# Moving a gate recurrence, weight conversions and one group's key and query transposes in an mLSTM and SwiGLU kernel

## The chip, the cores and the metric

One core of one Trainium2 chip runs the whole program. The metric is device microseconds of one execution; lower is better. TensorE (PE) multiplies, VectorE (DVE), ScalarE (ACT) and GpSimd (POOL) do the rest, and two engines issue transfers here: SyncE (SP) nearly all, ACT a few. "PEld" is the loading of stationary operands into PE, which overlaps PE's own work.

## The reference, cut to what matters

```python
# q, k, v, o_gate: (4, 8, 768, 40); i_gate, f_gate: (4, 8, 768)
for t in range(S):                                   # S = 768
    m_new  = np.maximum(f_gate[:, :, t] + m, i_gate[:, :, t])
    f_stab = np.exp(f_gate[:, :, t] + m - m_new)
    i_stab = np.exp(i_gate[:, :, t] - m_new)
    C = f_stab * C + i_stab * outer(v_t, k_t)        # 40 x 40 per head
    n = f_stab * n + i_stab * k_t
    y[:, :, t] = sigmoid(o_gate_t) * (C @ q_t) / max(|n . q_t|, 1)
x = y laid out as (3072 tokens, 320)
out = (silu(x @ w_gate) * (x @ w_val)) @ w_out       # d_ff = 1536
```

The weights arrive as 64-bit floats and are brought to 32 bits inside the kernel.

## The kernel before

The sequence of 768 steps is cut into six groups of 128 steps (`NG`, `g` or `n` counts them). For each group the recurrent cell is computed in parallel form, which gives 512 token rows (4 batches of 128), and these go through the SwiGLU block: `hidden(g, m)` makes chunk m of 12 of the hidden layer (20 recorded matrix products into two PSUM banks, a Silu on ACT, a product on DVE, line L640), and `project` or `project_all` multiplies by `w_out`. The cell of group n+1 is computed between the chunks of group n: a table `slots` says what is emitted after which chunk. The schedule is manual: each engine runs its instructions in the order in which the Python code emits them. An engine that waits holds back all that was emitted later for it.

The names that the change and the prediction touch:

- **Gates of the later groups.** `late_sums` (L269) makes running sums of the forget gate and the differences to the input gate; `late_maxima` (L276) makes the running maxima `M_sb` by a scan, then the decays `step1` (an Exp on ACT, L281), and stores `M_sb` to HBM as `M_dram`. From there `weights_load` spreads it into `w_sb`. `late_turns` (L604) transposes the results into `g_T`, `e_T`; `decay_rows`, `decay` make the table `dec`.
- **Weights.** `piece_load(p)` (L136) loads piece p of `PIECES`: pieces 0 and 1 hold chunk 0 and chunk 1, pieces 2 to 6 hold chunks 2-3, 4-5, 6-7, 8-9, 10-11, pieces 7 to 9 hold `w_out`. A gate half goes by SP, a value half by ACT (L142). Landing places are two `raw` buffers, or for some pieces `h_sb` and `wo_sb`, not yet used. `convert(j)` is `scale` (two ACT instructions, L186 and L188), `join` (two DVE instructions, L195, L196) and `rounded` (L203, on POOL or DVE). `ahead[m]` lists the chunks converted while chunk m is made; j = 12 to 17 are pieces of `w_out`.
- **Scores and states.** `turn` (L297) transposes keys and queries of a group on PE, with copies out of PSUM by ACT and DVE. `turn_squares` (L314) does the same for groups 3 to 5 by DVE, from tiles of 32x32 that `load_squares` (L305) fetches in 16 small transfers. `weights_sub`, `weights_mask`, `weights_exp` prepare the decay weights, `weigh_values` the weighted values, `sig` the output gate. `add` (L343) makes the sums of keys and values of a 64-step half, `next_state` (L355) decays the state on POOL and adds the sum on DVE. `attend` (L362) and `gather` use it.
- **PSUM.** Two sets of four banks: "cell" for all cell work, "gen" for `hidden` and the projection. `hidden` of chunk m+2 can start only when Silu and product of chunk m have emptied their banks.
- **Transfer counters.** Transfers issued by SP and ACT take turns on eight completion counters. An issue first waits for the landing of the transfer that last used its counter, if its engine has not yet seen that landing.

The end of the first group's work is emitted so (L736 to L742): `project_all(0, after)`, in which the table `after` says what follows which m, and then

```python
    weights_exp(0)
    weights_exp(1)
    sig(0)
    sig(1)
    weigh_values(G, 0)
    weigh_values(G, 1)
```

`result` copies each projection from PSUM by ACT to one of two `z_sb` buffers (L644), and SP stores it.

Of the kernel before, what the change touches and what calls it, by code (L numbers as in the profile page):

```python
# [18 lines left out]
L = 128  # L19
# [5 lines left out]
def kernel(  # L25
# [47 lines left out]
    def flat(t):  # L73
        return t.rearrange("p c t -> p (c t)")
# [61 lines left out]
    def piece_load(p, home=None):  # L136
        kind, m, n = PIECES[p]
        if kind == "gv":
            a, d = NKC, n * 128
            src = [(slice(i * HP, (i + 1) * HP), w[:, m * 128:(m + n) * 128].rearrange("(c p) f -> p c f", p=HP))  # L140
                   for i, w in enumerate((moe_w_gate, moe_w_val))]
            queues = (nc.sync, nc.scalar)  # L142
        else:
            a, d = n, DM
            src = [(slice(0, 128), moe_w_out[m * 128:(m + n) * 128].rearrange("(a p) d -> p a d", p=128))]
            queues = (nc.sync,)
        if src[0][1].dtype == F32:
# [12 lines left out]
        for (r, w), queue in zip(src, queues):  # L160
            queue.dma_start(out=raw[r].rearrange("p (a d) -> p a d", a=a), in_=w.bitcast(U32))  # L161
# [107 lines left out]
    def late_sums():  # L269
        nc.vector.tensor_tensor_scan(flat(f_sb), flat(keep1), flat(f_sb), 0.0, op0=ALU.mult, op1=ALU.add)  # L270
        nc.gpsimd.memset(step1, 0.0)
        nc.vector.tensor_sub(i_sb, i_sb, f_sb)
        nc.vector.tensor_copy(step1[:, 0:1, 0:1], f0[0:BH, end].unsqueeze(1))
        nc.vector.tensor_copy(step1[:, 1:, 0:1], f_sb[:, 0:NL - 1, last])

    def late_maxima():  # L276
        nc.vector.tensor_tensor_scan(flat(M_sb), flat(step1), flat(i_sb), M0[0:BH, end], op0=ALU.add, op1=ALU.max)
        nc.vector.tensor_add(m_in[:, 0:1], M0[0:BH, end].unsqueeze(1), f0[0:BH, end].unsqueeze(1))
        nc.vector.tensor_add(m_in[:, 1:], M_sb[:, 0:NL - 1, last], f_sb[:, 0:NL - 1, last])
        nc.vector.tensor_sub(step1, m_in.to_broadcast([BH, NL, SUB]), M_sb)  # L280
        nc.scalar.activation(step1, step1, AF.Exp)  # L281
        nc.sync.dma_start(out=M_dram, in_=flat(M_sb))

    M_dram = tc.dram_tile([BH, S - L], F32, name="M_dram")

# [54 lines left out]
    def small(name, n=UA):  # L340
        return bank(name)[:, 0:n * D1].rearrange("p (a d) -> p a d", d=D1)

    def add(P):  # L343
        ps = [small("add") for _ in range(2)]
        for a in range(UA):
            for i, two in QUAD:
                h = P * UH + 2 * a + two
                nc.tensor.matmul(ps[i][half(two), a, :], lhsT=k_sb[half(i), h, :], rhs=vw_sb[half(i), h, :],  # L348
                                 start=True, stop=True)
        return ps  # L350

    def state(s):
        return C_ring[s % 3]

    def next_state(s, P, ps):  # L355
        a = slice(P * UA, (P + 1) * UA)
        nc.gpsimd.tensor_tensor(state(s + 1)[:, a], state(s)[:, a],  # L357
                                dec[:, s - 2, a].unsqueeze(2).to_broadcast([128, UA, D1]), op=ALU.mult)
        nc.vector.tensor_tensor(state(s + 1)[:, a], state(s + 1)[:, a], ps, op=ALU.add)  # L359
# [215 lines left out]
    first_scores(1)
    sig(0)
    sig(1)
    piece_load(2, h_sb[:, NH - NKC:])
    piece_load(3, wo_sb)
    burn(3)  # L580
    first_own(2)
    first_own(3)
# [87 lines left out]
    def do_weigh(P):  # L670
        weigh(P, live.pop(("sp", P)))

    def do_add():
        for P in range(2):
            live["add", P] = add(P)

    def do_state(s, P):
        for i, ps in enumerate(live.pop(("add", P))):
            next_state(s + i, P, ps)
# [15 lines left out]
    def load_all(dst, a, n):  # L695
        for P in range(2):
# [3 lines left out]


    on_vector = (9, 10, 11)
    ahead = {m: [m + 2] for m in range(NFC)}
    ahead[8] = [10, 11]
    ahead[9] = []
    slots = {
        0: [run(first_state, 1, A), run(load_all, k_sb, k, 1), run(load_all, q_sb, q, 1)],
        1: [run(late_maxima), run(piece_load, 6, h_sb[:, NH - NKC:])],
        2: [run(weights_load, 1), run(load_all, v_sb, v, 1), run(decay_rows)],
        3: [run(late_turns)],  # L710
        4: [run(decay)],
        5: [run(turn, 0, (A, A), (A, V))],
        6: [run(turn, 1, (A, A), (A, V)), run(piece_load, 7)],
        7: [run(weights_sub, 1, 0), run(weights_sub, 1, 1), run(weights_mask, 0), run(weights_mask, 1)],
        8: [run(weights_exp, 0), run(weights_exp, 1), run(weigh_values, G, 0), run(weigh_values, G, 1),
            run(piece_load, 8)],
        9: [run(do_scores), run(do_weigh, 0), run(do_weigh, 1), run(load_all, o_sb, o_gate, 1)],
        10: [run(do_add), run(do_state, 2, 0), run(do_state, 2, 1)],
        11: [run(do_attend, 1, 0), run(do_gather, 1, 0, False), run(piece_load, 9)],
    }  # L720
    for m in range(NFC):
        hidden(0, m, [run(convert, j, V if j in on_vector else None) for j in ahead[m]])
        for f in slots.get(m, ()):
            f()
    after = {
        0: [run(do_attend, 1, 1), run(convert, 14), run(sig, 0), run(sig, 1), run(do_gate, 0)],
        1: [run(do_gather, 1, 1), run(weights_load, 2), run(load_all, v_sb, v, 2)],
        2: [run(do_divide, 1, 0), run(convert, 15)],
        3: [run(do_divide, 1, 1), run(load_all, k_sb, k, 2), run(load_all, q_sb, q, 2), run(load_all, o_sb, o_gate, 2)],
        4: [run(convert, 16), run(seam, 1, 0, (A, V, A, V))],  # L730
        5: [run(seam, 1, 1, (A, V, A, V))],
        6: [run(convert, 17)],
        8: [run(weights_sub, 2, 0), run(weights_mask, 0)],
        9: [run(weights_sub, 2, 1), run(weights_mask, 1)],
    }
    project_all(0, after)  # L736
    weights_exp(0)
    weights_exp(1)
    sig(0)
    sig(1)  # L740
    weigh_values(G, 0)
    weigh_values(G, 1)  # L742
    early_scope.close()
    late = ctx.enter_context(tc.tile_pool(name="late", bufs=1))
    xTs.append(late.tile([128, NKC, TW], F32, name="xT1"))
# [6 lines left out]
    for g in range(1, NG):  # L752
        n, f = g + 1, g + 2
        slots = {m: [] for m in range(NFC)}
        if n < NG:
            slots[0] = [run(turn, 0, (A, V), (A, V))] if n == 2 else [run(turn_squares, q_sq, qT)]
            slots[1] = [run(turn, 1, (A, V), (A, V))] if n == 2 else [run(turn_squares, k_sq, kT)]
            if n == 2:
                slots[1].append(run(nc.gpsimd.memset, q_sb, 0.0))
            slots[3] = [run(do_scores), run(do_weigh, 0)]  # L760
            slots[4] = [run(do_weigh, 1)]
            slots[5] = [run(do_add), run(do_state, 2 * n, 0)]
            slots[6] = [run(do_state, 2 * n, 1)]
# [58 lines left out]
```

## Time and profile before

| | us |
|---|---|
| median of 3 runs | 568.58 |
| lowest, highest | 565.74, 569.22 |
| the profiled execution | 567.32 |
| its span in the profile | 565.2 |
| DVE busy | 225.4 |
| ACT busy | 139.3 |
| POOL busy | 103.8 |

The profile is one execution; the 2.1 us between its time and its span lie outside the recorded instructions. A group of instructions is given as line, engine, operation, output<-inputs and count. "Idle before" is the time an engine stood still just before an instruction, with what released it. PE is busy nearly everywhere in this kernel, so the short stretches in which it isn't, and those in which it is busy longer than the same work takes elsewhere, are what to look for.

### The profile page before, as it was taken

To read this page: it belongs to the slowest core of one execution; us is meant where nothing else is said; L and a number is where in the kernel's file an instruction comes from. 1 tells how busy PE (TensorE), PEld (TensorE's weight loads), DVE (VectorE), ACT (ScalarE), POOL (GpSimd) and SP (SyncE) were. 2 spreads that over 40 slices of the span, in tenths; PEclk is the share of its full clock that TensorE was granted. 3 is DMA by queue.
4 is the path that set the end of the run, shared out by engine and by line. 5 is a ranking of instruction groups with operands and counts; after the bars stand their busy time and mean duration, and the time that the engine had idled before them with its cause. 6 is when DMAs were issued, how large, how long until landed. Compare 5 with 4: busy or idle time off the path is not lost.

```text
span 565.2 us, 11653 instructions
## 1 busy us (share of the span) xinstructions
PE 554.4 (98%) x5055; PEld 322.7 (57%) x5056; DVE 225.4 (40%) x379; ACT 139.3 (25%) x208; POOL 103.8 (18%) x95
## 2 busy tenths in 40 slices
PE   8997999999999999999999999999999999999997
PEld 4855545665555476455566455567455557544475
DVE  5775576880334531434612424613432631011100
ACT  4365446435401015110104201104211010111100
POOL 2132344555211123002105001206001100000000
PEclk9999999999999999999999999999999999999999
DMA  9999991594362395353295253196000131000000
GB/s 124 182 271 187 179 264 22 151 152 95 41 79 26 50 148 110 44 53 49 38 149 111 41 66 49 31 145 110 24 2 2 26 59 46 12 1 1 1 23 24
DMA packets 211227, 45.05 MB, mean 80 GB/s; under 512 B 201736, under 2 KB 206344, under 8 KB 211176
## 3 DMA queue, kind: packets, MB, share of 16 engines
q1 hardware_dynamic: 208596, 40.14, 44.5%
q10 hardware_dynamic: 2580, 4.16, 3.3%
q8 instruction: 40, 0.66, 0.5%
q14 instruction: 11, 0.09, 0.1%
HBM read 35.03 MB, written 4.01 MB: 69 GB/s over the span
## 4 chain that ended last, share of the span: by engine, by line
PE 84%; DMA 5%; SPq 4%; DVE 3%; ACT 2%; POOL 1%; issue 1%; ACTq 0%; DVEq 0%; POOLq 0%
PE gv_ps L634 49%; PE o_ps L650 23%; PE o_ps L657 5%; SPq L113 3%; DMA raw<-in_moe_w_val_dram 3%; DMA h_sb<-in_moe_w_gate_dram 2%; PE intra L372 2%; PE inter L367 2%; PE sp L327 1%; PE add L348 1%; DVE wgv_sb L196 1%; DVE wgv_sb L195 1%; POOL C L357 1%; PE tp_kq L292 0%; SPq L161 0%
## 5 line engine op out<-in xcount | busy, mean ns | idle before, releaser
L634 PE MATMUL gv_ps<-xT,wgv_sb 64*128 64x512 f32 x1440 | 320.7, 596 | 4.5 <-POOL wgv_sb L203 3.6
L634 PEld LDWEIGHTS gv_ps<-xT,wgv_sb 64*128 64x128 f32 x1440 | 144.5, 188 | 158.9 <-issue 149.4
L640 DVE TENSOR_TENSOR h_sb<-sg,gv_ps 128x512 f32<-128x512 f32 x72 | 49.4, 687 | 227.7 <-ACT sg L639 227.7
L650 PE MATMUL o_ps<-wo_sb,h_sb 128*128 128x320 f32 x480 | 130.5, 433 | 0.0
L650 PEld LDWEIGHTS o_ps<-wo_sb,h_sb 128*128 128x128 f32 x480 | 90.8, 190 | 41.0 <-issue 3.8
L639 ACT ACTIVATE sg<-gv_ps 128x512 f32<-128x512 f32 x72 | 43.0, 597 | 261.3 <-PE gv_ps L634 261.3
L357 POOL TENSOR_TENSOR C<-C,dec 128x328 f32<-128x328 f32 x20 | 14.5, 737 | 146.6 <-DVE C L359 146.6
L446 POOL TENSOR_SCALAR_AFFINE_SELECT w_sb<-w_sb 64x1024 f32<-64x1024 f32 x20 | 28.2, 1409 | 58.9 <-DVE w_sb L441 58.0
L644 ACT COPY z_sb<-o_ps 128x320 f32<-128x320 f32 x24 | 10.2, 424 | 101.8 <-PE o_ps L650 90.7
L657 PE MATMUL o_ps<-wo_sb,h_sb 128*128 128x320 f32 x96 | 26.9, 437 | 0.0
L393 POOL TENSOR_TENSOR o_sb<-o_sb,y_sb 128x640 f32<-128x640 f32 x10 | 14.2, 1425 | 61.7 <-DVE y_sb L384 61.7
L441 DVE TENSOR_TENSOR w_sb<-g_T,w_sb 128x1024 f32<-128x1024 f32 x10 | 13.1, 1354 | 26.8 <-DMA w_sb<-M_dram 26.8
L657 PEld LDWEIGHTS o_ps<-wo_sb,h_sb 128*128 128x128 f32 x96 | 17.9, 190 | 7.2
L416 DVE STREAM_TRANSPOSE xT<-x_sq 128x640 f32<-128x640 f32 x16 | 12.5, 821 | 23.5 <-DMA x_sq<-x_sb 23.5
L384 DVE TENSOR_TENSOR y_sb<-y_sb,intra 64x328 f32<-64x328 f32 x40 | 19.7, 493 | 0.7
L203 POOL TENSOR_TENSOR wgv_sb<-wgv_sb,low 128x640 int32<-128x640 int32 x8 | 13.3, 1667 | 29.2 <-DVE wgv_sb L196 29.2
L337 POOL TENSOR_TENSOR vw_sb<-v_sb,w_sb 128x656 f32<-128x656 f32 x10 | 13.0, 1318 | 8.6 <-issue 6.4
L367 PEld LDWEIGHTS inter<-C,qT 64*64 64x64 f32 x640 | 10.2, 134 | 7.3 <-issue 6.1
L359 DVE TENSOR_TENSOR C<-C,add 128x328 f32<-128x328 f32 x20 | 9.9, 493 | 10.5 <-POOL C L357 10.5
L203 POOL TENSOR_TENSOR wo_sb<-wo_sb,low 128x640 int32<-128x640 int32 x6 | 10.2, 1706 | 15.0 <-DVE wo_sb L196 10.5
L334 DVE TENSOR_TENSOR w_sb<-sp,w_sb 128x512 f32<-128x512 f32 x20 | 12.7, 682 | 0.2 <-issue 0.2
L372 PE MATMUL intra<-v_sb,w_sb 64*64 64x41 f32 x640 | 12.3, 228 | 0.4 <-DVE C L359 0.3
(127 smaller groups left out, 353.1 us busy)
## 6 DMA issues: line engine op xcount, KB each, us to landing
w_sb<-M_dram SPq DMA_DIRECT2D x10, 512.0 KB, 6.8
x_sq<-x_sb SPq DMA_DIRECT2D x128, 40.0 KB, 2.0
k_sb<-in_k_dram SPq DMA_DIRECT2D x12, 320.0 KB, 5.9
v_sb<-in_v_dram SPq DMA_DIRECT2D x12, 320.0 KB, 7.0
o_sb<-in_o_gate_dram SPq DMA_DIRECT2D x12, 320.0 KB, 5.6
raw<-in_moe_w_out_dram SPq DMA_DIRECT2D x3, 1280.0 KB, 7.8
out_dram<-z_sb SPq DMA_DIRECT2D x24, 160.0 KB, 1.8
q_sb<-in_q_dram SPq DMA_DIRECT2D x6, 320.0 KB, 8.7
```

Source lines behind the costliest of these rows:

```text
L113: nc.sync.dma_start(out=dst[:, heads(P), 0:D], in_=tokens(a, c, P))
L203: (eng or nc.gpsimd).tensor_tensor(dst, dst, lo, op=ALU.add)
L357: nc.gpsimd.tensor_tensor(state(s + 1)[:, a], state(s)[:, a], dec[:, s - 2, a].unsqueeze(2).to_broadcast([128, UA, D1]), op=ALU.mult)
L367: nc.tensor.matmul(inter[two][half(i), a, :], lhsT=qT[half(two), P * UA + a, half(i)], rhs=state(2 * n + i)[half(two), P * UA + a, :], sta ...
L372: nc.tensor.matmul(intra[i][half(c), a, :], lhsT=w_sb[half(i), h, :], rhs=v_sb[half(i), h, :], start=True, stop=True)
L384: nc.vector.tensor_tensor(t, t, intra[i][half(c)], op=ALU.add)
L446: nc.gpsimd.affine_select(w, w, compare_op=ALU.is_ge, fill=NEG, base=0, pattern=[[0, UH], [1, SUB]], channel_multiplier=-1)
L634: nc.tensor.matmul(ps[i], lhsT=wgv_sb[half(i), m, PAIRS[kc][i] if g < 2 else kc, :], rhs=x[half(i), kc, :], start=(kc == 0), stop=(kc == N ...
L639: nc.scalar.activation(sg, ps[0], AF.Silu)
L640: nc.vector.tensor_tensor(hid(g, m), sg, ps[1], op=ALU.mult)
L650: nc.tensor.matmul(p, lhsT=hid(g, m)[:, ts(u, L)], rhs=wo_sb[:, m, :], start=(m == 0), stop=(m == NFC - 1))
L657: nc.tensor.matmul(ps[u], lhsT=hid(g, m)[:, ts(u, L)], rhs=wo_sb[:, m, :], start=(m == 0), stop=(m == NFC - 1))
```

## The change

It moves work between slots and queues and changes how one group's keys and queries are transposed:

1. `late_sums` and a cut `late_maxima` (up to the scan) move ahead, among the first group's cell steps; a new `late_decay` with the Exp stands where `late_sums` stood; the difference `i_sb` moves from DVE to POOL; the store to `M_dram` is issued after piece 3.
2. Piece 6's value half is issued by SP. `ahead` converts chunks 7 to 10 one step earlier and takes the pair 10, 11 apart; `late_turns`, `decay`, `weights_sub`, `weights_mask` move up by a slot.
3. Group 2 ("third group") no longer uses `turn`: `q` and `k` come by `load_squares` (16 transfers each) and `turn_squares`; `k_sb` is still loaded, for `add`.
4. `add` for groups 2 to 5 uses 40 stationary columns in place of 64, and `next_state` then adds two ranges of 40 partitions. The decay of the first half is made ahead of the sums.
5. `weights_exp`, `sig` and `weigh_values` of group 2 move from behind `project_all(0)` into it (`after[9]`, `after[10]`).

```diff
-            queues = (nc.sync, nc.scalar)
+            queues = (nc.sync, nc.scalar if p < 6 else nc.sync)
...
-        nc.vector.tensor_sub(i_sb, i_sb, f_sb)
+        nc.gpsimd.tensor_sub(i_sb, i_sb, f_sb)
+
+    def late_maxima():
         nc.vector.tensor_copy(step1[:, 0:1, 0:1], f0[0:BH, end].unsqueeze(1))
         nc.vector.tensor_copy(step1[:, 1:, 0:1], f_sb[:, 0:NL - 1, last])
-
-    def late_maxima():
         nc.vector.tensor_tensor_scan(flat(M_sb), flat(step1), flat(i_sb), M0[0:BH, end], op0=ALU.add, op1=ALU.max)
+
+    def late_decay():
...
         nc.scalar.activation(step1, step1, AF.Exp)
-        nc.sync.dma_start(out=M_dram, in_=flat(M_sb))
...
+    def feats(i):
+        return slice(i * SUB, i * SUB + D)
...
-    def add(P):
+    def add(n, P):
         ps = [small("add") for _ in range(2)]
+        rows, w = (half, DP) if n == 1 else (feats, D)
...
-                nc.tensor.matmul(ps[i][half(two), a, :], lhsT=k_sb[half(i), h, :], rhs=vw_sb[half(i), h, :],
+                nc.tensor.matmul(ps[i][rows(two), a, :], lhsT=k_sb[half(i), h, 0:w], rhs=vw_sb[half(i), h, :],
...
-    def next_state(s, P, ps):
+    def decayed(s, P):
         a = slice(P * UA, (P + 1) * UA)
         nc.gpsimd.tensor_tensor(state(s + 1)[:, a], state(s)[:, a],
...
-        nc.vector.tensor_tensor(state(s + 1)[:, a], state(s + 1)[:, a], ps, op=ALU.add)
+
+    def next_state(s, P, ps):
+        a = slice(P * UA, (P + 1) * UA)
+        for r in (slice(0, 128),) if s < 4 else (feats(0), feats(1)):
+            c = state(s + 1)[r, a]
+            nc.vector.tensor_tensor(c, c, ps[r], op=ALU.add)
...
     first_own(0)
+    late_sums()
...
     piece_load(1)
+    late_maxima()
     first_own(1)
     first_values(1)
+    first_scores(1)
     first_x(1)
-    first_scores(1)
...
     piece_load(3, wo_sb)
+    nc.sync.dma_start(out=M_dram, in_=flat(M_sb))
...
-    late_sums()
+    late_decay()
...
-    ahead = {m: [m + 2] for m in range(NFC)}
-    ahead[8] = [10, 11]
-    ahead[9] = []
+    ahead = {m: [m + 2] for m in range(4)}
+    ahead.update({4: [6], 5: [7, 8], 6: [9], 7: [10], 8: [11], 9: [], 10: [], 11: []})
...
-        1: [run(late_maxima), run(piece_load, 6, h_sb[:, NH - NKC:])],
-        2: [run(weights_load, 1), run(load_all, v_sb, v, 1), run(decay_rows)],
-        3: [run(late_turns)],
-        4: [run(decay)],
+        1: [run(piece_load, 6, h_sb[:, NH - NKC:]), run(decay_rows)],
+        2: [run(late_turns), run(weights_load, 1), run(load_all, v_sb, v, 1)],
+        3: [run(decay)],
...
-        7: [run(weights_sub, 1, 0), run(weights_sub, 1, 1), run(weights_mask, 0), run(weights_mask, 1)],
+        6: [run(turn, 1, (A, A), (A, V)), run(weights_sub, 1, 0), run(weights_mask, 0), run(piece_load, 7)],
+        7: [run(weights_sub, 1, 1), run(weights_mask, 1), run(nc.gpsimd.memset, q_sb, 0.0)],
...
+        9: [run(do_scores), run(do_weigh, 0), run(do_weigh, 1), run(do_decayed, 2), run(load_all, o_sb, o_gate, 1)],
+        10: [run(do_add, 1), run(do_state, 2), run(rounded, 12), run(load_squares, q_sq, q, 2)],
...
+    def early_squares(part):
+        if part == 0:
+            live["k_sq"] = conv.tile([128, 4 * NKC * 128], F32, name="raw")[:, 0:PP * L].rearrange("p (a t d) -> p a t d", a=PP, d=SQ)
+            nc.gpsimd.memset(live["k_sq"], 0.0)
+            load_squares(live["k_sq"], k, 2)
+        else:
+            turn_squares(live.pop("k_sq"), kT)
...
-        3: [run(do_divide, 1, 1), run(load_all, k_sb, k, 2), run(load_all, q_sb, q, 2), run(load_all, o_sb, o_gate, 2)],
+        3: [run(do_divide, 1, 1), run(load_all, o_sb, o_gate, 2), run(early_squares, 0)],
...
+        5: [run(seam, 1, 1, (A, V, A, V)), run(convert, 17), run(weights_sub, 2, 0), run(weights_mask, 0)],
+        7: [run(weights_sub, 2, 1), run(weights_mask, 1), run(load_all, k_sb, k, 2)],
+        8: [run(turn_squares, q_sq, qT)],
+        9: [run(weights_exp, 0), run(weights_exp, 1), run(weigh_values, G, 0), run(weigh_values, G, 1)],
+        10: [run(sig, 0), run(sig, 1)],
+        11: [run(early_squares, 1)],
     }
     project_all(0, after)
-    weights_exp(0)
-    weights_exp(1)
-    sig(0)
-    sig(1)
-    weigh_values(G, 0)
-    weigh_values(G, 1)
...
-            slots[0] = [run(turn, 0, (A, V), (A, V))] if n == 2 else [run(turn_squares, q_sq, qT)]
-            slots[1] = [run(turn, 1, (A, V), (A, V))] if n == 2 else [run(turn_squares, k_sq, kT)]
-            if n == 2:
-                slots[1].append(run(nc.gpsimd.memset, q_sb, 0.0))
+            if n > 2:
+                slots[0] = [run(turn_squares, q_sq, qT)]
+                slots[1] = [run(turn_squares, k_sq, kT)]
...
-            slots[5] = [run(do_add), run(do_state, 2 * n, 0)]
-            slots[6] = [run(do_state, 2 * n, 1)]
+            slots[4].append(run(do_decayed, 2 * n))
+            slots[5] = [run(do_add, n), run(do_state, 2 * n)]
```

More of the change, by code (lines that the diff above doesn't have):

```diff
@@ L671, in do_weigh, with do_add, do_state, do_decayed @@
         weigh(P, live.pop(("sp", P)))
-    def do_add():
+    def do_add(n):
         for P in range(2):
[L675 to L679, printed above, removed]
+            live["add", P] = add(n, P)
+    def do_state(s):
+        ps = [live.pop(("add", P)) for P in range(2)]
+        for i in range(2):
+            for P in range(2):
+                next_state(s + i, P, ps[P][i])
+                if i == 0:
+                    decayed(s + 1, P)
+    def do_decayed(s):
+        for P in range(2):
+            decayed(s, P)
     def do_attend(n, P):
@@ L702 @@
     on_vector = (9, 10, 11)
-    ahead = {m: [m + 2] for m in range(NFC)}
-    ahead[8] = [10, 11]
-    ahead[9] = []
+    ahead = {m: [m + 2] for m in range(4)}
+    ahead.update({4: [6], 5: [7, 8], 6: [9], 7: [10], 8: [11], 9: [], 10: [], 11: []})
     slots = {
         0: [run(first_state, 1, A), run(load_all, k_sb, k, 1), run(load_all, q_sb, q, 1)],
-        1: [run(late_maxima), run(piece_load, 6, h_sb[:, NH - NKC:])],
-        2: [run(weights_load, 1), run(load_all, v_sb, v, 1), run(decay_rows)],
-        3: [run(late_turns)],
-        4: [run(decay)],
+        1: [run(piece_load, 6, h_sb[:, NH - NKC:]), run(decay_rows)],
+        2: [run(late_turns), run(weights_load, 1), run(load_all, v_sb, v, 1)],
+        3: [run(decay)],
         5: [run(turn, 0, (A, A), (A, V))],
-        6: [run(turn, 1, (A, A), (A, V)), run(piece_load, 7)],
-        7: [run(weights_sub, 1, 0), run(weights_sub, 1, 1), run(weights_mask, 0), run(weights_mask, 1)],
+        6: [run(turn, 1, (A, A), (A, V)), run(weights_sub, 1, 0), run(weights_mask, 0), run(piece_load, 7)],
+        7: [run(weights_sub, 1, 1), run(weights_mask, 1), run(nc.gpsimd.memset, q_sb, 0.0)],
         8: [run(weights_exp, 0), run(weights_exp, 1), run(weigh_values, G, 0), run(weigh_values, G, 1),
             run(piece_load, 8)],
-        9: [run(do_scores), run(do_weigh, 0), run(do_weigh, 1), run(load_all, o_sb, o_gate, 1)],
-        10: [run(do_add), run(do_state, 2, 0), run(do_state, 2, 1)],
+        9: [run(do_scores), run(do_weigh, 0), run(do_weigh, 1), run(do_decayed, 2), run(load_all, o_sb, o_gate, 1)],
+        10: [run(do_add, 1), run(do_state, 2), run(rounded, 12), run(load_squares, q_sq, q, 2)],
         11: [run(do_attend, 1, 0), run(do_gather, 1, 0, False), run(piece_load, 9)],
@@ L721 @@
     for m in range(NFC):
-        hidden(0, m, [run(convert, j, V if j in on_vector else None) for j in ahead[m]])
+        first = [run(convert, j, V if j in on_vector else None) for j in ahead[m]]
+        first += {10: [run(scale, 12), run(join, 12)], 11: [run(convert, 13)]}.get(m, [])
+        hidden(0, m, first)
         for f in slots.get(m, ()):
             f()
+    def early_squares(part):
[5 more added lines that the diff above has]
+            turn_squares(live.pop("k_sq"), kT)
     after = {
@@ L728 @@
         2: [run(do_divide, 1, 0), run(convert, 15)],
-        3: [run(do_divide, 1, 1), run(load_all, k_sb, k, 2), run(load_all, q_sb, q, 2), run(load_all, o_sb, o_gate, 2)],
+        3: [run(do_divide, 1, 1), run(load_all, o_sb, o_gate, 2), run(early_squares, 0)],
         4: [run(convert, 16), run(seam, 1, 0, (A, V, A, V))],
[L731 to L734, printed above, removed]
+        5: [run(seam, 1, 1, (A, V, A, V)), run(convert, 17), run(weights_sub, 2, 0), run(weights_mask, 0)],
[4 more added lines that the diff above has]
+        11: [run(early_squares, 1)],
     }
     project_all(0, after)
-    weights_exp(0)
-    weights_exp(1)
-    sig(0)
-    sig(1)
-    weigh_values(G, 0)
-    weigh_values(G, 1)
     early_scope.close()
```

## The prediction

> **What bounds the kernel now.** I read the page's chain of waits first, then the waits of PE alone, then PE's timeline around each wait, then stages with their clock. The chain by engine:
>
> ```profile
> PE 84%; DMA 5%; SPq 4%; DVE 3%; ACT 2%; POOL 1%; issue 1%; ACTq 0%; DVEq 0%; POOLq 0%
> ```
>
> In order of time its last 420 us (from 146.05) are PE alone, in rounds of 86.7 us; the rest of the 16% lies before 146. So only that first part, and PE's own work, can give time. PE's waits in 0 to 200 us (waiter, releaser: total, times, longest; after 200 there is none):
>
> ```profile
> PE gv_ps L634 <- POOL wgv_sb L203: 3.6, 1, 3.6
> PE burn L459 <- DVE warm L220: 1.2, 1, 1.2
> PE gv_ps L634 <- DVE h_sb L640: 0.5, 1, 0.5
> ...
> PE tp_kq L292 <- ACT kT L117: 0.4, 1, 0.4
> PE intra L372 <- DVE C L359: 0.3, 1, 0.3
> PE tp_kq L292 <- DVE qT L119: 0.2, 1, 0.2
> ```
>
> The largest is chunk 4's wait for its weights. ACT's timeline (start, length) shows why they are late:
>
> ```profile
> 47.79 0.74 ACT L281 ACTIVATE keep<-keep 32x640 f32<-32x640 f32 x1 [3.01 <-DVE keep L280]
> 50.62 0.60 ACTq L161 DMA_DIRECT2D h_sb<-in_moe_w_val_dram  x1
> 51.33 0.78 ACT L186 ACTIVATE top<-wo_sb 128x640 f32<-128x640 f32 x1 [2.80 <-DMA raw<-in_moe_w_gate_dram]
> ```
>
> ACT issues piece 6's value half before it scales chunk 4, and that issue stood until piece 5's value half landed (34.09 + 16.45 = 50.54 in the chain). Chunk 4's data had landed at 42.1 (issue 25.72, 16.4 to landing). The wait costs more than itself; stages, with length, busy times, clock and DMA share:
>
> ```profile
> 51.60:55.20 3.60, 0.05 (x1) 0.00 (x0) 1.80 (x3) 3.57 (x5) 1.53 (x1) 1.00 1.30 172
> 55.20:58.00 2.80, 2.78 (x8) 2.26 (x10) 2.73 (x9) 1.90 (x4) 0.53 (x1) 0.61 1.25 162
> 58.00:61.70 3.70, 3.70 (x16) 2.48 (x12) 2.19 (x4) 1.06 (x3) 2.34 (x2) 0.84 1.22 140
> 61.70:87.90 26.20, 26.20 (x296) 13.80 (x295) 17.84 (x21) 14.39 (x23) 9.85 (x7) 1.00 1.02 218
> ```
>
> After the idle stretch the granted clock is 0.61, then 0.84, and chunk 4 takes 6.49 us where others take 4.40.
>
> [...]after 3.57 us the clock fell, after waits of 1 us it did not. [...]here 64 columns are recorded at 135 ns, 128 at 190, so less than proportional. [...]
>
> **The change part by part.**
>
> *Piece 6, conversions, decays moved ahead.* Without the issue at 50.62 and the Exp at 47.79, chunk 4 is scaled after Silu of chunk 1. From chunk 3's end (50.91) to chunk 5's start (62.17) are 11.26 us; needed are the gate transposes 0.73, `dec` 0.46, chunk 4 at 4.40: 5.59. **Gain 5.67.**
>
> *The head pays for it.* The store of `M_dram`, now between pieces 3 and 4, shifts all later transfers by one of the eight counters. In the instruction order of both programs with their waits I find two new stops on ACT. Piece 3's value half now waits for piece 0's gate half: landing 18.97 + 9.3 = 28.27, in place of an issue at 25.72. Behind it stand the copies of the first seam, which began at 27.18 and can now begin at 28.27 + 0.63 = 28.9. **Loss 1.7.** On DVE the two scans (1.47 and 2.51), two copies (0.29), and 4 score products ahead of `first_x(1)`, with about 1.6 us of old idle time before 20.5, push the gates and copies back about 1.5; that lies beside the 1.7. The difference on POOL (near `vw_sb` of the same size, 1.29) and the memset 0.62 fit before values at 19.67.
>
> Second, piece 5's value half, issued at 34.09, now waits for piece 3's gate half: 22.36 + 15.6 = 38.0. Behind it are Exp with its table (1.28 + 0.74), scaling of chunk 2 (1.5), the Silu table (1.28), Silu (0.60): 38.0 + 0.6 + 5.4 = 44.0, product on DVE 44.8, before 42.0. With the head's shift PE is through chunk 1 at 33.5 + 4.49 + 1.05 + 4.45 = 43.5 and needs the banks and weights (POOL ready about 44.4): **loss 1.1.** Scaling of chunk 4 then follows at 46.4 and ends on POOL near 50, needed 54.8. Later landings hold: q of group 1 lands at 61.5 and 62.9, wanted at 64 and 69; piece 6, two issues of 0.6 on SP behind the q loads (about 59), near 68, wanted near 72 (scaled after chunk 6).
>
> *DVE relieved around chunk 9.* Chunk 10 takes 6.06 us (87.92 to 93.98), 1.66 over 4.40: the product of chunk 8 stood behind `weights_sub` and two joins of 1.4 us slowed beside POOL. These are now spread over four slots. **Gain 1.66.** The decays made ahead free the sums' banks: attend takes 2.6 in place of 2.1. **Gain 0.5.** PE reaches the projection at 103.1 - (5.67 - 1.7 - 1.1 + 1.66 + 0.5) = 98.1.
>
> *Scores' weights ahead of the projection's end.* Exp and Sigmoid now stand before the `z_sb` copies on ACT. The masks on POOL do not come earlier: they hang on conversion 17, which follows the seam copies, and end at 125.80 + 5.76 = 131.56, 28.5 after the projection's start. Then 1.0 (second Exp) + 1.28 + 1.36 + 0.96 (two copies) = 33.1, where the next hidden chunk began at 30.5. **Loss 2.3**, taken a little under the 2.6 because the first copy releases the first product. DVE's products and SP's stores stand behind those copies.
>
> *Group 2 without PE transposes.* Two chunks with two turns take 12.43 us (133.62 to 146.05); alone 2 x 4.39. **Gain 3.65** (1.98 transposes, the rest waits). DVE's four square transposes (1.22 each) and POOL's memsets (1.8) fall in the projection, where DVE idles 16 us before 143.4. On SP, the q squares (16 issues, 8.57) stand ahead of piece 9, issued at 97.25 and then idle-waiting; they end near 93. The k squares (9.07) begin after divide and memset, 16.8 after the start, then k_sb's two issues (4.0): free at 30, just when the first store is due. I cost SP at nothing, up to 2.
>
> *Sums of 40 columns.* An `add` takes 2.01 us for 64 sums, 126 ns per quarter of the array; scores with 64 moving columns instead of 41 take 2.02, so moving columns don't set it. First-group products with 128 stationary columns take 235 ns each; between, 1.7 ns a column. With 40: 126 - 24 x 1.7 = 85, but I take 95 as loading isn't all of it: 1.5 us. **Gain 4 x 0.48 = 1.9.** The trace shows no 40-column load: bounds are 0 (if issuing 128 records sets it) and 4 x 0.75 = 3.0; a loss needs more instructions, and there are as many. On DVE four more additions of 0.49 per group stand before the product of chunk 6, which has 4.4 us: hidden.
>
> **Sum:** 5.67 - 1.7 - 1.1 + 1.66 + 0.5 - 2.3 + 3.65 + 1.9 = 8.3 us. The profiled execution took 567.32, which gives 559.0; the median of the runs is 1.3 above that execution. I say **559.5**.
>
> **Rivals.**
> 1. *Fewer stops than I charge*: the counters' landings come earlier, masks finish earlier. Without the head's 2.8 and the 2.3, 40 columns at 3.0 in place of 1.9: gain 14.5; half of it, gain 11 to 13: about 556. For it: all three rest on landings or order, not on work. Against: the landing times are in the trace.
> 2. *The new wait at the projection's end slows the clock.* [...]it pays about 2 us of slow clock as at 55.2, and 40 columns bring nothing: gain 8.3 - 2 - 1.9 = 4.4, or 563. For it: 2.3 is not far from 3.57.
> 3. *The change does not do what it says*: chunk 4 still waits as another landing is late (value half of piece 3, issued 2.6 later), with a 3.5 us wait and slow clock again: gain 8.3 - 5.6 = 2.7, about 564.5. Against: 10 us lie between 42.1 and 52.
> 4. *Slower: SP becomes the bound behind the projection.* The squares' 16 issues, k_sb and the stores are one queue; `z_sb` has two buffers, so copies 3 and 4, Silu and then PE hang on the first store. While DMA is full an issue can take long: one k load of group 1 stood 10.8 us. Should the 18 issues ahead of the stores take 36 us in place of 13, the stores come 23 late; 1.6 of slack and the 4.4 of one chunk lie against it, and PE loses 17, so 8.3 - 17: slower by 9, 576. It outweighs all gains from 14 us of delay on. Against: in the projection SP's loads took 2.0 to 2.7 us each.
>
> **How the numbers follow.** Chances: my case 0.50, rival 1 0.15, rival 2 0.19, rival 3 0.08, rival 4 0.08. About 1% (5.7 us) is what this kernel's measurement can tell from no change, so faster than 562.9 counts as faster: my case, rival 1 and nearly half of rival 2, 0.73; same 0.19; slower 0.08. The range 554.8 to 565 holds my case with its bounds (0 to 3.0 for sums, 2 for SP, about 1.5 either way for the head), most of rivals 1 to 3, and leaves out rival 4 and the outer ends.
>
> **What would show it.** PE's wait for POOL at chunk 4 gone and the clock 1.00 from 33 to 130; the first chunk at 33.5, not 31.8; ACT standing until 38 before the Exp; a PE wait of about 1 us at chunk 2; chunk 10 at 4.4 us; hidden chunk 0 of the second group behind an ACT copy; no transposes of k and q after 134; `add` of groups 2 to 5 at about 1.5 us. I am wrong if PE waits over 3 us anywhere after 31, if the stores begin over 3 us behind the projection's end, or if `add` keeps 2.0.

## The result, and the profile after

| | before | after |
|---|---|---|
| median of the runs, us | 568.47 (4 runs) | 560.02 (4 runs) |
| lowest, highest | 565.74, 569.22 | 559.30, 560.83 |
| the profiled execution | 567.32 | 560.56 |
| its span | 565.2 | 558.7 |
| ratio, 95% interval | | 0.9861 [0.9833, 0.9889] |

The change saves 8.45 us, 1.4%. In two later sets the same kernel stood at 0.988 [0.9854, 0.9906] and 0.9861 [0.9834, 0.9889], 7.1 and 8.2 us under the kernel before.

PE's longest waits in the first 200 us of the kernel after (waiter, releaser: total, times, longest):

```profile
PE gv_ps L648 <- DVE wgv_sb L207: 2.1, 1, 2.1
PE gv_ps L648 <- ACT z_sb L658: 2.0, 1, 2.0
PE gv_ps L648 <- POOL wgv_sb L207: 1.2, 1, 1.2
...
```

The 3.6 us at chunk 4 are gone. In their place stand three waits, and the prediction had named each: the first chunk (2.1), the first hidden chunk of the second group behind the `z_sb` copies (2.0), chunk 2 (1.2). Behind the last of them PE waits for nothing up to 200 us. PE's timeline has the places of the first and third, and chunk 4 (start, length):

```profile
33.80 4.56 PE L648 MATMUL gv_ps<-xT,wgv_sb 64*128 64x512 f32 x20 [2.11 <-DVE wgv_sb L207]
...
45.13 4.80 PE L648 MATMUL gv_ps<-xT,wgv_sb 64*128 64x512 f32 x20 [1.21 <-POOL wgv_sb L207]
...
55.55 6.71 PE L648 MATMUL gv_ps<-xT,wgv_sb 64*128 64x512 f32 x30
```

Chunk 4 starts at 55.55 without a wait, and chunk 5 follows at 60.0 inside the same row. Chunk 5 began at 62.17 before. ACT's timeline shows the price in the head:

```profile
28.79 0.60 ACTq L165 DMA_DIRECT2D wo_sb<-in_moe_w_val_dram  x1
29.43 1.07 ACT L121 COPY xT<-tp_x 128x512 f32<-128x512 f32 x2 [2.99 <-PE tp_x L562]
30.39 0.81 ACT L190 ACTIVATE top<-raw 128x640 f32<-128x640 f32 x1
...
38.67 0.60 ACTq L165 DMA_DIRECT2D raw<-in_moe_w_val_dram  x1
39.30 1.28 ACT L287 ACT_TABLE_LOAD   x1 [3.94 <-DMA wo_sb<-in_moe_w_gate_dram]
40.60 0.74 ACT L287 ACTIVATE keep<-keep 32x640 f32<-32x640 f32 x1
```

Piece 3's value half is issued at 28.79 (25.72 before), so the first seam copies begin at 29.43 and the first chunk's scaling at 30.39. The store of the maxima, which the code emits behind this issue, had been issued by SP at 24.2. Piece 5's value half stands until 38.67, and the Exp with its table, chunk 2's scaling and Silu all queue behind it. The two traces name the counter (a semaphore of the program) of every transfer: eight are in use, for 44 transfers each in the kernel after, and none of the 344 issues that use one again starts before the transfer that last used it has landed (before: none of 314). Piece 3's value half has the counter of piece 0's gate half, landed at 28.71; before, that of an `o_gate` load, landed at 25.05. Piece 5's value half has that of piece 3's gate half, landed at 38.60; before, that of piece 2's gate half, landed at 34.02.

At the projection's end ACT's timeline reads:

```profile
126.76 1.06 ACT L461 ACTIVATE w_sb<-w_sb 128x1024 f32<-128x1024 f32 x1 [1.35 <-POOL w_sb L457]
127.83 1.28 ACT L464 ACT_TABLE_LOAD   x1
129.13 1.36 ACT L464 ACTIVATE o_sb<-o_sb 128x640 f32<-128x640 f32 x2
130.40 0.73 ACT L658 COPY z_sb<-o_ps 128x320 f32<-128x320 f32 x2
132.76 0.89 ACT L658 COPY z_sb<-o_ps 128x320 f32<-128x320 f32 x2 [1.64 <-DMA out_dram<-z_sb]
```

PE has finished the projection at 128.9; the banks come free with the copies at 130.85. The stages of that place, cut where the clock changes, with length, busy times of PE, PEld, DVE, ACT and POOL, the granted clock, DMA share and GB/s:

```profile
127.61:131.02 3.41, 1.44 (x6) 0.74 (x5) 2.28 (x2) 3.38 (x6) 2.83 (x3) 1.00 1.46 151
131.02:134.44 3.42, 3.42 (x9) 2.79 (x11) 0.00 (x0) 1.73 (x4) 2.12 (x3) 0.50 0.42 137
134.44:137.85 3.41, 3.41 (x19) 2.97 (x17) 0.08 (x1) 1.11 (x2) 0.00 (x0) 1.00 0.78 140
```

After an idle time of 1.97 us the clock is 0.50 for exactly one such stage: 9 products are recorded in it where the next has 19. This half-speed slot costs about 1.7 us, an estimate (half of 3.41), and the prediction's main sum had no term for it.

### The profile page after: what moved, and what is told of

It is laid out like the page before. It is cut to its first block, busy times and chain, and to the rows that moved or that the text cites. A ratio compares the mean times of both kernels' runs of the same rounds, so it can differ in the third digit from the quotient of the medians.

```text
span 558.7 us, 11598 instructions
## 1 busy us (share of the span) xinstructions
PE 548.1 (98%) x4992; PEld 320.6 (57%) x4992; DVE 235.8 (42%) x394; ACT 135.7 (24%) x203; POOL 106.7 (19%) x97
## 4 chain that ended last, share of the span: by engine, by line
PE 86%; SPq 5%; DMA 3%; DVE 2%; POOL 1%; ACT 1%; issue 1%; ACTq 0%; POOLq 0%
PE gv_ps L648 55%; PE o_ps L664 23%; SPq L117 3%; DMA wo_sb<-in_moe_w_gate_dram 3%; PE sp L332 2%; PE inter L378 2%; PE intra L383 2%; PE add L354 1%; SPq L316 1%; SPq L165 1%; DVE y_sb L395 1%; POOL wo_sb L207 1%; POOL w_sb L457 0%; PE tp_kq L297 0%; DVE wo_sb L200 0%
## 5 line engine op out<-in xcount | busy, mean ns | idle before, releaser
L648 PEld LDWEIGHTS gv_ps<-xT,wgv_sb 64*128 64x128 f32 x1440 | 147.1, 188 | 157.1 <-issue 146.1
L370 DVE TENSOR_TENSOR C<-C,add 40x328 f32<-40x328 f32 (+1 forms) x36 | 17.7, 493 | 1.3 <-POOL C L363 0.4
L398 DVE TENSOR_SCALAR den<-den 128x16 f32<-128x16 f32 x10 | 12.3, 1228 | 0.3
L461 ACT ACTIVATE w_sb<-w_sb 128x1024 f32<-128x1024 f32 x10 | 10.5, 1055 | 7.4 <-POOL w_sb L457 7.4
```

The source lines that it names most:

```text
L370: nc.vector.tensor_tensor(c, c, ps[r], op=ALU.add)
L648: nc.tensor.matmul(ps[i], lhsT=wgv_sb[half(i), m, PAIRS[kc][i] if g < 2 else kc, :], rhs=x[half(i), kc, :], start=(kc == 0), stop=(kc == N ...
```

## The experiments

Eleven runs were made, in three sets, two of them of the kernel after again; each set has its own runs of the kernel before. Below, chunk (g, m) is hidden chunk m of group g, both counted from 0.

### One part alone: piece 6's value half by SP

In the kernel before:

```diff
-            queues = (nc.sync, nc.scalar)
+            queues = (nc.sync, nc.scalar if p < 6 else nc.sync)
```

> The kernel before with one change: piece 6's value half is issued by SP, not ACT. Theory (the issue that stands on ACT until another transfer lands makes chunk 4 late, and the idle time also costs clock): chunk 4 is scaled at about 48.5 in place of 51.33, PE's wait at chunk 4 falls from 3.6 to about 0.8 us, the clock behind it stays 1.00, chunk 4 takes 4.4 in place of 6.5, and the span falls by 4.9 us (2.8 + 2.1). Rival (the slow clock does not come from the wait): the wait falls, chunk 4 still takes 6.5, 2.8 us. Rival (the data land late anyway): nothing changes.

563.46 us, ratio 0.995 [0.9919, 0.9981]. PE's timeline of this run:

```profile
43.67 8.32 PE L634 MATMUL gv_ps<-xT,wgv_sb 64*128 64x512 f32 x38
51.92 0.49 PE L608 MATMUL tp_g<-ident,i_sb 32*128 32x32 f32 x5
52.26 0.47 PE L608 MATMUL tp_g<-ident,keep 32*128 32x32 f32 x5
52.66 4.56 PE L634 MATMUL gv_ps<-xT,wgv_sb 64*128 64x512 f32 x20
57.15 0.53 PE L621 MATMUL dec_ps<-dec_r,halves 32*128 32x160 f32 x2
57.61 4.56 PE L634 MATMUL gv_ps<-xT,wgv_sb 64*128 64x512 f32 x20
```

Chunk 3 ends at 51.99 and chunk 5 starts at 57.61: 5.62 us in place of 11.26. The single word in the queue choice carries the whole of the first term: the wait, and the half-speed slot that followed it. The Exp stayed where it was (47.78 on ACT) and did no harm, so moving it was not needed for this. The medians are only 3.1 us apart (566.58 to 563.46), less than the 4.9 expected of the span; in the profiled execution the head was 1.5 us worse than before (first chunk at 33.29, with a half-speed slot from 26.2).

### The head: the store of the maxima behind piece 5

In the kernel after:

```diff
     piece_load(3, wo_sb)
-    nc.sync.dma_start(out=M_dram, in_=flat(M_sb))
...
     piece_load(5)
+    nc.sync.dma_start(out=M_dram, in_=flat(M_sb))
```

> The changed kernel with one move: the store to M_dram is issued behind piece 5 in place of behind piece 3, so that pieces 3 to 5 have the same transfer counters as in the kernel before. Theory (the store's place shifts the counters and stops ACT twice): ACT issues piece 3's value half near 25.8 in place of 28.8 and piece 5's near 34.1 in place of 38.7, the first hidden chunk starts near 31.9 in place of 33.8, PE's wait at chunk 2 falls below 1 us, and the span falls by about 2.3 us. Rival (the scans on VectorE hold the head back): ACT issues earlier, but the first chunk still starts after 33 and the span falls by less than 0.8 us.

559.07 us, ratio 0.9875 [0.9831, 0.9918]. ACT's timeline of this run:

```profile
23.95 0.63 ACTq L165 DMA_DIRECT2D wo_sb<-in_moe_w_val_dram  x1
...
35.55 0.60 ACTq L165 DMA_DIRECT2D raw<-in_moe_w_val_dram  x1
36.19 1.28 ACT L287 ACT_TABLE_LOAD   x1 [0.66 <-ACT low L192]
```

Neither issue stands any more (28.79 and 38.67 in the kernel after), and PE's wait at chunk 2 is gone: from the first chunk's start to chunk 2's end are 14.4 us, where the kernel after has 16.1. So the two stops of ACT do come from the store's place among the counters. The other profiles agree: in all eight with the store behind piece 3 the value half of piece 3 is issued within 0.2 us of the landing of piece 0's gate half, in the three with the store moved 2.0 to 2.8 us before it. But the first chunk still began at 33.94: in this execution the clock was 0.50 from 27.7 to 31.1, and nothing was won there. Two runs below have the store moved and the clock at 1.00, and there the first chunk began at 33.38 and 33.19, as in the third run of the kernel after (33.20): its scaling waited 1.1 us for piece 0's gate half, which landed near 29.8. So no run shows the first chunk back at 31.8. The rival's scans did not hold it: the last products with the output gate on DVE ahead of it started at 27.82 in the kernel after and at 28.17 before. The span fell by 1.5 us against the kernel after, 2.3 expected; this set has no run of the kernel after, and the medians do not separate the two.

### The projection's end: Sigmoids behind the copies

In the kernel after:

```diff
-        10: [run(sig, 0), run(sig, 1)],
...
     project_all(0, after)
+    sig(0)
+    sig(1)
```

> The changed kernel with one move: the two Sigmoids of group 2 are emitted behind the projection (behind its four copies on ACT) in place of within it. Theory (Sigmoid with its table, 2.6 us ahead of the copies, makes PE wait 1.97 us at the second group's first chunk, and that idle time costs clock): the wait goes, the clock stays 1.00, the first two chunks take 4.4 each in place of 6.3 and 4.3, and the span falls by 3.8 us. Rival (SP's queue of small transfers and stores holds the copies): PE waits in chunk 1 of the group in place of chunk 0, and the span falls by less than 1 us.

558.85 us, ratio 0.9863 [0.9822, 0.9904]. The wait of 2.0 us and the half-speed slot behind it are gone; from the projection's start to scores of group 2 are 48.50 us (51.54 after). The whole did not show it: the span was 559.7, 1.0 above the kernel after, where 3.8 less was expected. In this execution the head was worse: piece 0's gate half landed near 31.0, PE waited 2.15 us for the seam copies and 1.16 for the first chunk, and the clock was 0.50 from 32.1 to 42.3.

Both edits in one kernel:

> The changed kernel with both moves: the store behind piece 5 and the Sigmoids behind the projection. Theory: the two stops are in different stages and add up: 2.3 + 3.8 = 6.1 us less than the changed kernel, a span near 552.6. Rival (PE's time gained at the head is given back at the projection's end, where the masks on GpSimd and the squares' transfers do not come earlier): about 4 us less.

558.39 us, ratio 0.9844 [0.9807, 0.988]. The clock was 1.00 throughout the profiled execution. Its span of 557.4 is 1.3 under the kernel after; neither the 6.1 of the theory nor the rival's 4 came. Part of the gain came back as a later Silu, as ACT's timeline of it shows:

```profile
133.92 0.79 ACT L658 COPY z_sb<-o_ps 128x320 f32<-128x320 f32 x2 [4.20 <-DMA out_dram<-z_sb]
134.73 1.28 ACT L464 ACT_TABLE_LOAD   x1
136.03 1.36 ACT L464 ACTIVATE o_sb<-o_sb 128x640 f32<-128x640 f32 x2
137.41 1.28 ACT L653 ACT_TABLE_LOAD   x1
138.70 1.08 ACT L653 ACTIVATE sg<-gv_ps 128x512 f32<-128x512 f32 x2
```

The first Silu is at 138.70, 8.6 us behind the start of chunk (1,0), so the four chunks take 18.8 us. The third copy stood 4.20 us for the landing of the first store, 1.64 in the kernel after: SP issued that store at 129.42, 0.7 us behind the last load of `k_sb`, in the kernel after 3.6 behind it. The medians of these three runs lie within 0.7 us of each other, and what the clock does was not yet clear.

### The clock: the kernel after again, and with PE kept busy in the wait

> The kernel after, once more, so that the other runs of this set stand beside it on the same chip. If the stages repeat: PE idle about 2 us at the projection's end behind the z copies, then a clock well under 1.00 for some 6 us (0.53 and 0.93 in the first execution), hidden chunk (1,0) 6.3 us in place of 4.4, scores of group 2 at about 150. If the slow clock was an accident of one execution: the same wait, but clock 1.00 and chunk (1,0) at 4.4 us. The granted clock in the head (26 to 33 us) may differ from execution to execution.

The second edit puts five products that nobody reads into the wait at the projection's end:

```diff
     project_all(0, after)
+    burn(5)
```

> The kernel after, with 5 idle bf16 products of 0.379 us (1.9 us) emitted on PE between the projection and hidden chunk (1,0): the wait for the z copies stays as long as it was, but PE is not idle in it. Theory (the idle time of 1.97 us brings the slow clock): clock 1.00 from 129 to 142, hidden chunk (1,0) 4.4 us in place of 6.3, from the projection's start to scores of group 2 some 1.8 us less than in the kernel after (51.5 to 49.7). Rival (the clock falls there for another reason, for instance the load of the transfers or the step from projection to hidden chunks): clock under 0.9 all the same, no change in the stage. If the products' bank is late, a wait of their own and a loss of up to 2 us.

560.14 us, ratio 0.988 [0.9854, 0.9906], and 560.07, ratio 0.9877 [0.9851, 0.9902]: no difference. The five products took 1.24 us together and left a wait of 0.90; the clock behind it was 1.00. But the expected contrast failed in the control. In the repeated kernel after, the wait at the projection's end was there (1.98 us) and the clock stayed at 1.00; a wait of 2.18 us at chunk 2 was followed by 0.50 instead. Its stages, cut at the edges of the half-speed slot and in steps of 3.41 us from there:

```profile
43.77:47.18 3.41, 1.44 (x7) 1.31 (x9) 1.82 (x4) 3.40 (x6) 1.54 (x1) 1.00 1.06 366
47.18:50.59 3.41, 3.41 (x11) 2.67 (x9) 3.34 (x8) 1.68 (x3) 1.54 (x1) 0.50 1.42 159
129.10:132.51 3.41, 2.08 (x8) 1.14 (x6) 2.37 (x2) 3.38 (x4) 3.08 (x3) 1.00 1.43 163
132.51:135.92 3.41, 2.77 (x13) 2.03 (x15) 0.00 (x0) 1.74 (x5) 2.69 (x3) 1.00 0.57 121
```

The wait at chunk 2 lies almost whole in one slot (PE busy 1.44 of 3.41); the one at the projection's end is cut by a slot's edge into 1.33 and 0.64. The first was followed by a slot at 0.50, the second by one at 1.00. I took from this that PE's idle time within one slot (1.97 against 1.33 us), not the length of the wait (2.18 against 1.98), goes with the clock of the next. The spare products could then help only in executions where one slot holds most of the wait.

The third run of the kernel after was to test this:

> The kernel after once more, beside the combination on the same chip. What is asked of it is the granted clock in slots of 3.41 us: if the clock of a slot is set by how long PE was idle in the slot before it, then a slot with more than 1.8 us of recorded PE idle is followed by one at 0.50, and one with under 1.7 us is not, wherever the waits of about 2 us (first chunk, chunk 2, projection's end) lie in this execution. Rival (any wait near 2 us at the projection's end slows the clock, those in the head do not): 0.50 behind the projection's end and nowhere else. Median about 560.

558.31 us, ratio 0.9861 [0.9834, 0.9889]. The rival fell: PE idled 1.98 us at the projection's end and 1.84 at the first chunk, and the clock was 1.00 all through. The theory missed as well. Where a profile has no half-speed slot, the edges here are an estimate: behind the last instruction the clock goes to 0.50, in the kernel after at 557.69, 125 x 3.413 us behind the edge at 131.03, in the kernel before at 564.39, 149 x 3.413 behind the one at 55.80. In the third run it does so at 557.00. Counted back from there in steps of 3.413, one slot begins at 31.35 and another at 126.92:

```profile
31.35:34.76 3.41, 1.56 (x9) 0.97 (x10) 2.34 (x5) 2.77 (x5) 0.00 (x0) 1.00 1.04 282
34.76:38.18 3.42, 3.42 (x30) 1.63 (x29) 3.01 (x4) 0.00 (x0) 1.53 (x1) 1.00 1.07 265
126.92:130.34 3.42, 1.60 (x6) 0.78 (x5) 2.22 (x2) 3.39 (x5) 3.24 (x3) 1.00 1.48 153
130.34:133.75 3.41, 3.25 (x15) 2.38 (x17) 0.00 (x0) 1.72 (x5) 2.05 (x3) 1.00 0.31 101
...
556.60:557.00 0.40, 0.00 (x0) 0.00 (x0) 0.00 (x0) 0.00 (x0) 0.00 (x0) 1.00 0.00 0
557.00:557.40 0.40, 0.00 (x0) 0.00 (x0) 0.00 (x0) 0.00 (x0) 0.00 (x0) 0.50 0.09 20
```

PE idled 1.85 and 1.82 us in these two slots, more than the 1.8 expected to suffice, and the next slots are at 1.00. Over all thirteen profiles, with all slots from 28 to 148 us in which PE idled over 1.2 us while the clock was 1.00 (idle times to about 0.02):

| kernel | slot from | PE idle in it | clock of the next slot |
|---|---|---|---|
| before | 52.39 | 2.83 | 0.50 |
| spare products | 42.83 | 2.77 | 0.50 |
| store behind piece 5 | 126.65 | 1.99 | 0.50 |
| after | 127.61 | 1.97 | 0.50 |
| after, again | 43.77 | 1.97 | 0.50 |
| 64 columns (below) | 128.41 | 1.92 | 0.50 |
| after, third run | 31.35 | 1.85 | 1.00 |
| after, third run | 126.92 | 1.82 | 1.00 |
| Sigmoids behind copies | 28.65 | 1.80 | 0.50 |
| after | 32.03 | 1.76 | 1.00 |
| after, third run | 41.59 | 1.44 | 1.00 |
| group 2 by turns (below) | 129.06 | 1.34 | 1.00 |
| after, again | 129.10 | 1.33 | 1.00 |
| both moves, later Sigmoids (below) | 31.86 | 1.33 | 1.00 |
| 64 columns (below) | 29.42 | 1.32 | 1.00 |
| conversions as before (below) | 126.65 | 1.26 | 1.00 |
| after | 42.27 | 1.21 | 1.00 |

In these profiles 1.92 us and more were followed by half speed in the next slot, in all six cases, and 1.76 and less were not, in all eight. Between 1.80 and 1.85 it went both ways, so idle time alone does not decide there. The one slot at 1.80 that was followed by 0.50 also differs in what came next: the clock stayed at 0.50 for three slots, though PE idled only 0.86 and 0.67 us in the first two of them. This is a count over these executions; no run moved a wait on purpose, which is hard to do, as the slots' position differs from execution to execution (edges at 131.03 in the kernel after, 132.51 in it again).

### The sums with 64 columns

In the kernel after:

```diff
-        rows, w = (half, DP) if n == 1 else (feats, D)
+        rows, w = half, DP
```

> The kernel after, with 64 stationary columns in the sums of all groups, as before; the state's additions stay split in two ranges of 40 partitions. Theory (the columns set the time of the sums): each add of groups 2 to 5 takes 2.01 us in place of 1.53, so each round of a group is 0.48 longer and the whole 1.9 us. Rival (issue of 128 records sets it, and the gain came from elsewhere): add stays at 1.5 and the rounds at their length.

562.19 us, ratio 0.9919 [0.9892, 0.9946], 2.05 above the kernel after in the same set. The sums of group 2, first in this run, then in the kernel after:

```profile
160.52 2.08 PE L354 MATMUL add<-vw_sb,k_sb 64*64 64x41 f32 x128
```

```profile
160.96 1.60 PE L354 MATMUL add<-vw_sb,k_sb 64*40 64x41 f32 x128
```

With 64 stationary columns the sums take 2.08 us, with 40 they take 1.60: 0.48 us for each of four groups, 1.9 in all. The theory's number was met.

### Group 2 by PE's transposes

The small tiles of group 2 are left out, its keys and queries are loaded whole, and `turn` stands behind chunks (1,0) and (1,1) again. In the kernel after, in part:

```diff
...
+            slots[0] = [run(turn, 0, (A, V), (A, V))] if n == 2 else [run(turn_squares, q_sq, qT)]
+            slots[1] = [run(turn, 1, (A, V), (A, V))] if n == 2 else [run(turn_squares, k_sq, kT)]
...
```

> The kernel after, with group 2's keys and queries again loaded whole and transposed on PE behind hidden chunks (1,0) and (1,1), without the small tiles. Theory: these two chunks and two turns take 2.0 us more for the transposes and up to 1.7 more for waits for the copies, so scores of group 2 come 2.0 to 3.7 us later than in the kernel after. Rival (DVE's square transposes and SP's 32 small transfers cost as much as the turns): the projection starts or ends earlier by as much, and scores of group 2 come at the same time, within 0.7 us.

560.31 us, ratio 0.9886 [0.9863, 0.9908]; the medians show nothing. The stage does: from chunk (1,0) to scores of group 2 (130.40 to 150.18) are 19.78 us, against 17.69 in the third run of the kernel after, at clock 1.00 in both. PE's timeline of that run:

```profile
130.50 17.76 PE L648 MATMUL gv_ps<-xT,wgv_sb 64*128 64x512 f32 x80 [1.98 <-ACT z_sb L658]
148.19 2.10 PE L332 MATMUL sp<-qT,kT 64*64 64x64 f32 x128
```

So the transposes are worth 2.1 us, the lower end of what I expected. The kernel before took 21.0 for the same stage (133.62 to 154.62). The remaining 1.2 us are not due to the small tiles, which this run leaves out. ACT's timelines suggest the cause: before, Exp, Sigmoid and three table loads stood ahead of the first copy of k (143.27, 9.65 us behind chunk (1,0)'s start); with Exp and Sigmoid in the projection it comes at 135.76, 5.36 behind it, even with `turn`. No run takes this part alone.

### The conversions as before

In the kernel after:

```diff
-    ahead = {m: [m + 2] for m in range(4)}
-    ahead.update({4: [6], 5: [7, 8], 6: [9], 7: [10], 8: [11], 9: [], 10: [], 11: []})
+    ahead = {m: [m + 2] for m in range(8)}
+    ahead.update({8: [10, 11], 9: [], 10: [], 11: []})
```

> The kernel after with the conversions of chunks 7 to 11 in the slots where the kernel before had them. Theory (the spreading relieves DVE around chunk 9): chunk 10 is late again, a PE wait of about 0.5 us for the product of chunk 8 and 1.66 us more from chunk 9's end to the sums, so the sums of group 1 start 0.5 to 1.7 us later after scores of group 1 than in the kernel after (6.5 us behind the start of the scores there, 8.1 in the kernel before). Rival (the moved weights_sub and masks alone relieved it): the distance stays at 6.5.

559.05 us, ratio 0.9883 [0.985, 0.9916]. From scores of group 1 to the sums are 6.96 us (83.09 to 90.05); the kernel after has 6.51, the kernel before 8.11. The spreading is worth 0.45 us, just under the range expected; the larger part of chunk 10's relief comes from the other edits (weights and masks a slot earlier, the decays made ahead), which were not taken apart. Of the joins of chunks 10 and 11 in the kernel before, those that ran beside the masks on POOL took 1.44, 1.63 and 1.43 us; with POOL idle the same two instructions took 0.43 to 0.50 and 0.83.

### A version that beats both

Both moves, and the Sigmoids a little later, where ACT waits for PE anyway:

In the kernel after, with the store behind piece 5:

```diff
-        10: [run(sig, 0), run(sig, 1)],
...
+            if n == 2:
+                slots[1] = [run(sig, 0), run(sig, 1)]
```

> The kernel after with the store of the later gates' maxima behind piece 5, and both Sigmoids of group 2 moved out of the projection to behind hidden chunk (1,1), where ACT waits about 4 us for the next Silu. Theory: no stop of piece 5's value half at chunk 2 (PE wait there under 0.5), no wait at the projection's end, and Silu of chunk (1,0) directly behind the z copies, so that the four chunks (1,0) to (1,3) take 17.6 us in place of 18.9 in the run with both moves; from the projection's start to scores of group 2 48.3 us (49.6 there, 49.9 in the kernel after where its clock stayed at 1.00, 51.5 where it fell). Whole: 1 to 3 us under the kernel after, about 558. Rival: the two table loads and the Sigmoids (3.9 us) make Silu of chunk (1,2) late, a PE wait of up to 1.3 us there takes the gain back; whole equal to the run with both moves within 0.5.

555.83 us, ratio 0.9821 [0.9796, 0.9847]; the kernel after on the same chip 558.31. All its runs (555.18 to 556.91) lie below all of the kernel after's (557.98 to 558.45). PE's timeline:

```profile
129.21 17.54 PE L648 MATMUL gv_ps<-xT,wgv_sb 64*128 64x512 f32 x80
146.68 2.09 PE L332 MATMUL sp<-qT,kT 64*64 64x64 f32 x128
```

No wait in front, and the four chunks take 17.5 us (17.6 expected). From the projection's start (98.12) to scores are 48.56, expected 48.3. ACT's timeline shows the Sigmoids between two Silus, with 3.4 us to spare before the next:

```profile
138.09 0.60 ACT L653 ACTIVATE sg<-gv_ps 128x512 f32<-128x512 f32 x1 [2.63 <-PE gv_ps L648]
138.71 1.28 ACT L464 ACT_TABLE_LOAD   x1
140.00 1.36 ACT L464 ACTIVATE o_sb<-o_sb 128x640 f32<-128x640 f32 x2
141.38 1.28 ACT L653 ACT_TABLE_LOAD   x1
142.68 0.60 ACT L653 ACTIVATE sg<-gv_ps 128x512 f32<-128x512 f32 x1
146.68 0.60 ACT L653 ACTIVATE sg<-gv_ps 128x512 f32<-128x512 f32 x1 [3.40 <-PE gv_ps L648]
```

A wait of 1.75 us at the first chunk is left. It is not the stop that moving the store took away, for ACT's copies come at 27.60; behind them ACT waits for piece 0's gate half:

```profile
29.80 0.79 ACT L190 ACTIVATE top<-raw 128x640 f32<-128x640 f32 x1 [1.13 <-DMA raw<-in_moe_w_gate_dram]
```

## Why the prediction held, point by point

The forecast was 559.5, the median 560.02. So close an agreement is in part luck: in three sets the medians of the two kernels lay 7.1 to 8.45 us apart. "After" is its profiled execution; "third run" is the same kernel in an execution with the clock at 1.00 throughout.

| term of the sum | predicted | measured | from |
|---|---|---|---|
| chunk 4's wait and slow clock | +5.67 | +5.64 | piece 6 alone: 11.26 to 5.62 |
| the head | -1.7 | -2.0; third run -1.4 | first chunk at 33.80, 33.20; before 31.83 |
| chunk 2 | -1.1 | -1.2; third run -1.4 | PE's wait |
| chunk 10 and attend | +2.16 | +2.2 | scores of group 1 to projection: 17.21 to 15.02 |
| `z_sb` copies late | -2.3 | -1.7 | projection's start to chunk (1,0): 30.56 to 32.24 |
| group 2 without turns | +3.65 | +3.3; after +1.7 | chunk (1,0) to scores: 21.0 to 17.69, 19.30 |
| sums of 40 columns | +1.9 | +1.9 | 2.08 to 1.60, four groups |
| the span | +8.3 | +6.5; third run +8.6 | 565.2 to 558.7, 556.6 |

**What held.** The mechanisms and nearly all sizes. The two stops on ACT came from the shift of the counters, as read from the order of instructions, and moving the store took them away; that the first chunk then comes earlier is not shown. The masks on POOL did not come earlier (they ended 28.1 us behind the projection's start, 28.5 foreseen), so ACT's copies were late, as foreseen. None of the three signs of being wrong appeared: the longest wait of PE after 31 us was 2.1 us, the stores began 2.0 behind the projection's end, and `add` fell to about 1.5.

**The one step that failed** is in the line "`z_sb` copies late" and in rival 2: I charged the wait alone, though the profile before leaves open what the clock does between waits of about 1 us and the 3.57 us behind which it fell. That 2.3 us would leave it at 1.00 was an estimate of mine that no run had shown, and the runs went against it: 1.92 to 1.99 us of idle time within one slot of 3.41 us were followed by 0.50, in all four slots that had them. In the profiled execution this came at the projection's end (19.30 in place of 17.69 for the next four chunks), and that is 1.6 of the 2.1 us between the gains of 6.5 and 8.6; in the third run, with the same wait, it did not: an edge, by the estimate above, left 1.82 us of it in one slot. The fall of the clock in rival 2 came, behind 1.97 us and at 1.6 us where 2 was charged; its second half, sums without gain, did not come.

**Credits given to the wrong part.** Of the 3.65 for group 2 only 2.1 belong to the transposes; the other 1.2 seem to belong to Exp and Sigmoid moved out of the way, an edit that I had entered as a loss alone. And of the 1.66 at chunk 10 the spread conversions bring 0.45. The totals of these stages were right, their division was not.

**Costed at nothing.** SP was, rightly for this kernel. The k squares took 11.2 us in place of the 9.07 assumed, and SP was still free 3.6 us ahead of the first store (130.83), as the copies were late too. Where the copies come earlier, the third one waits longer for that store's landing (4.20 us above). Rival 4's queue thus existed, but far from the 14 us of delay at which it would have decided. Rivals 1 and 3 did not occur: all stops came, and chunk 4 did not wait.

**Open.** The head differs most between executions: piece 0's gate half landed at 26.0 to 31.0 us in the thirteen profiles (28.3 in the kernel before), which no edit here explains.

## What to carry to other kernels

Here a store added to queues that share completion counters shifted the waits of two issues on another engine (28.79 for 25.72 us, 38.67 for 34.09), so list what each issue must now wait for, and put a store that nobody needs soon behind the loads that others wait for. When work is moved off one wait, ask what stands behind it on the new engine: here a table switch with two Sigmoids ahead of the copies out of PSUM cost 1.7 us, and two chunks later, where that engine idles, it cost nothing (PE's four chunks took 17.54 us). Price a stall of PE by its length and by the clock after it (here 3.41 us at 0.50 behind some waits of 2 us, none behind others), and judge an edit of 1 to 2 us by its stage, with the clock of that stage beside it, not by medians that differ by as much from one execution to the next.

## What the hardware showed that I had not expected

- **The clock had two values, 1.00 and 0.50, and stood at 0.50 for 3.41 us at a time.** So in nine of the thirteen profiles; in one it was 10.24 us, three times as long, and three have 1.00 throughout up to 140 us or more. Readings such as 0.61 and 0.84 in the prediction's stages are windows that straddle an edge: the slot at 0.50 there is 55.80 to 59.22. Within an execution the edges lay at whole multiples of 3.413 us (47.18 - 26.70 = 6 x 3.413), and elsewhere in the next execution.
- **The clock was also 0.50 where no idle time stood before it.** In five profiles this was so in the slot from about 26 to 31 us. The slot ahead was filled by first-group products with 41 moving columns and PEld busy 3.35 to 3.41 of 3.41 us. Full loads alone did not bring it in the run with piece 6 alone: there the slot from 15.96 has PEld busy 3.41 of 3.41, half of its products are transposes with 128 moving columns, and the next slot is at 1.00. What sets the clock there is not shown.
